# A two-byte shift in the weight conversion, and token parts of 384 and 512 in place of 448 and 448

## The chip, the cores and the metric

The kernel runs on one core of a Trainium2 chip, as one launch. The metric is the device time of that launch in microseconds (us), the median of several runs. The engines are TensorE (PE in the profile, its weight loads PEld), VectorE (DVE), ScalarE (ACT), GpSimd (POOL) and the DMA queues, most of them issued by SyncE (SP).

## The reference

Causal attention over 2 batches, 12 heads, 448 tokens and 64 columns a head is followed by two feed-forward blocks on 768 columns. Cut to what matters:

```
attn = softmax(causal(q @ k.T / 8)) @ v            # [2, 448, 768] after joining the heads
xk, xr = mixes of attn with attn of the token before (mu_k, mu_r)
k = max(xk @ w_k, 0); r = sigmoid(xr @ w_r)        # w_k [768, 1024], w_r [768, 768]
x = r * ((k * k) @ w_v)                            # w_v [1024, 768]
h = max(x @ w_in, 0)
out = (h * sigmoid(conv3(h))) @ w_out
```

The five weight matrices and `conv_w` arrive as doubles, in 64-bit words, and are narrowed to floats on the chip; all other inputs are floats.

## The kernel before

Each product of the two blocks is made of three matmuls: both operands are split into a high and a low part, and `mm3` (L64) adds high by high, high by low and low by high. The weights come slice by slice, 128 output columns wide, with all input rows (128 partitions, 768 or 1024 elements). Each slice goes through the steps of `narrow` (L132), which turn a double into a float: `a` (ACT, the high word as a float, its absolute value), `b` (a clamp, on DVE or POOL), `c` (a shift and a mask, DVE, L142), `d` (sign and top exponent bit of the high word are put in, DVE, L144) and `e` (the three top bits of the low word are put in, DVE, L146). Then `h` (ACT) and `l` (DVE or POOL) split the float. In the profile a slice's tiles are `wr1raw`, `wr1c` and `wr1hl` for slice 1 of `w_r`, and so on; there are 36 slices, and `conv_w` is narrowed in the same way as one small tile.

The token axis has 896 tokens, two batches of 448. A PSUM bank holds 512 columns. The products with `w_r` (six slices) and with the first two slices of `w_k` take the tokens by batch, `TOK` (L213): two parts of 448, each in a bank of its own. All later products of the first two matrices and those with `w_in` take them as `HALF` (L672), 512 and 384. The final product with `w_out` has 384 columns a matmul.

The order of the work on PE, ACT, DVE and POOL is written out by hand in two lists, `ORDER` (L500) and `LATE` (L712); each engine works its own entries in that order. Between the two lists (L636 to L710: the rest of `w_k`, all of `w_v`) a planner, which estimates what each instruction costs, orders the work. In `ORDER`, `j:kqT`, `j:sc`, `j:T`, `j:V` are PE's four steps of attention for head pair j (0 to 11; 0 to 5 are batch 0), and what stands between them on the other engines is copies (`kC`, `C`), scores out of PSUM (`red`), exponentials (`exp`), sums and norms (`rec`, `norm`) and the mixes (`mP`, `mD`, `mH`, `mL`, which make `xr`). `w1:d` is step `d` of weight slice 1. `pr1.0.5` is the product of `w_r` slice 1, token part 0, input chunk 5: three matmuls. It needs `xr` of that chunk, which the head pair of that number in each batch makes. `sr1.0` copies the finished bank out. `E0` to `E3` are the two first slices of `w_k` with two parts each, six chunks of three matmuls. So `w_r` has 6 x 6 x 3 = 108 matmuls in each part, and E has 36 in each.

The products of part 0 of `w_r` slices 1, 2, 0 and, in part, 3 stand between the steps of attention; the rest of `w_r` and E follow when attention is through. The last four entries of attention on PE are `10:V.b`, `10:V.a`, `11:V.b`, `11:V.a`; the last, of 20 matmuls, needs `11:C.aX`, a copy of a bank on ACT, and `11:C.aY` on DVE; `11:V.b` needs `11:C.bY`, DVE's last copy. On ACT `w5:a`, `8:mH`, `9:mP.1`, `w4:a` and `9:mP.0` stand ahead of `11:C.aX`. Step `w0:h` on ACT needs `w0:e` on DVE, and `9:kC.q` on ACT needs the transposes `9:kqT`.

Of the kernel before, what the change touches and what calls it, by code (L numbers as in the profile page):

```python
# [9 lines left out]
F32 = mybir.dt.float32  # L10
I32 = mybir.dt.int32
I64 = mybir.dt.int64
F32R = mybir.dt.float32r
AF = mybir.ActivationFunctionType
ALU = mybir.AluOpType
# [4 lines left out]
def kernel(  # L20
# [18 lines left out]
    nc = tc.nc  # L39
    B, H, S, D = q.shape  # L40
    P = 128
# [7 lines left out]
    NT = B * S  # L49
    NC = DM // P  # L50
    NF = DFF // P
    NE = DM // P
# [11 lines left out]
    def mm3(ps_out, lh, ll, rh, rl, first, last, more=False):  # L64
        for i, (x, y) in enumerate(((lh, rh), (lh, rl), (ll, rh))):
            nc.tensor.matmul(  # L66
                ps_out, x, y, start=first and i == 0, stop=last and i == 2, skip_group_check=more,
            )
# [9 lines left out]
    def copy(eng, out_, in_):  # L78
        (nc.vector.tensor_copy if eng == "v" else nc.scalar.copy)(out_, in_)  # L79

    def split_h(eng, out_, in_):
        if eng == "p":
            nc.gpsimd.tensor_scalar(out_, in_, 1.0, 1.0, ALU.mult, ALU.mult)
        elif eng == "v":
            nc.vector.tensor_copy(out_, in_)
        else:
            nc.scalar.activation(out_, in_, AF.Copy)  # L87

    def split_l(eng, out_, x, h):
        e = nc.gpsimd if eng == "p" else nc.vector  # L90
        e.tensor_tensor(out_, x, f32(h), ALU.subtract)  # L91
# [18 lines left out]

    raws = Slots(wp, "wraw", 2, [P, NF * P], I64)
    wcs = Slots(wp, "wc", 2, [P, NF * P])
    whls = Slots(wp, "whl", 4, [P, 2, NF * P], F32R)
    mslots = Slots(mixp, "m", 3, [P, 512])
# [3 lines left out]
    def in_order(ins):  # L118
        if pinned[0]:
            tc.keep_in_program_order(ins)  # L120
# [5 lines left out]
    def as_float(bits):  # L126
        return struct.unpack("<f", struct.pack("<I", bits))[0]

    def as_int(bits):
        return bits - (1 << 32) if bits >> 31 else bits  # L130

    def narrow(step, dst, raw, eng="v"):  # L132

        lo, hi = raw[:, 0::2], raw[:, 1::2]
        d = dst.bitcast(I32)
        if step == "a":
            in_order(nc.scalar.activation(dst, hi.bitcast(F32), AF.Abs))
        elif step == "b":
            e = nc.gpsimd if eng == "p" else nc.vector
            e.tensor_scalar(dst, dst, as_float(HIGH), as_float(LOW), ALU.min, ALU.max)  # L140
        elif step == "c":
            nc.vector.tensor_scalar(d, d, 3, as_int(0x3FFFFFF8), ALU.logical_shift_left, ALU.bitwise_and)  # L142
        elif step == "d":
            nc.vector.scalar_tensor_tensor(d, hi, as_int(0xC0000000), d, ALU.bitwise_and, ALU.bitwise_or)  # L144
        else:
            nc.vector.scalar_tensor_tensor(d, lo, 29, d, ALU.logical_shift_right, ALU.bitwise_or)  # L146

    def load(w, m, name, rows, raw=None):

# [53 lines left out]
    def home(tag):  # L203
        return act if tag in early else late[0]

    def big(tag, name):
        return home(tag).tile([P, 2, NT], F32R, tag=tag, name=name)

    mixed = [act.tile([P, B, S], F32, tag=f"T{c}", name=f"mixed{c}") for c in range(NC)]
    xr = [big(f"Y{c}", f"xr{c}") for c in range(NC)]  # L210
    xk = {}
    sr = {}
    TOK = [slice(b * S, (b + 1) * S) for b in range(B)]  # L213

    free = [f"b{i}" for i in range(8)]
    held = {}

    def bank(key, uses):
        tag = free.pop(0)
        t = ps.tile([P, 512], F32, tag=tag, name=key, bufs=1)  # L220
        held[key] = [tag, t, uses]
        return t

    def used(key):
        h = held[key]
        h[2] -= 1
        if not h[2]:
            free.append(h[0])
        return h[1]
# [195 lines left out]
    def mix_h(dst, m, b, eng):  # L425
        split_h("p" if eng == "p" else "s", dst[:, 0, TOK[b]], m)

    def mix_l(dst, m, b, eng):
        split_l(eng, dst[:, 1, TOK[b]], m, dst[:, 0, TOK[b]])

    def products(out_, w, x, t, n, c):
        o = slice(c * P, c * P + P)
        mm3(out_, w[0][:, 0, o], w[0][:, 1, o], x[c][:, 0, t], x[c][:, 1, t], c == 0, c == n - 1)
# [21 lines left out]
    def first_steps(s):  # L455

        if s == "L":
# [4 lines left out]
            small["r"] = cr = t[:3 * NF, 2 * P:]  # L462
            in_order(nc.gpsimd.dma_start(out=cr.bitcast(I64), in_=conv_w.rearrange("t (f p) -> (t f) p", p=P)))
            small["c"] = t[:3 * NF, P:2 * P]
# [91 lines left out]
    slices = [Slice(e) for e in range(9)]  # L556
    ones = bank("W", 1)

    def keep_warm(n):
        for _ in range(n):  # L560
            nc.tensor.matmul(ones[:, :P], ident, ident, start=True, stop=True)  # L561

    def xr_products(e, b, c):
        if c == 0:
            bank(f"pr{e}_{b}", 1)
        products(held[f"pr{e}_{b}"][1][:, :S], [slices[e].t], xr, TOK[b], NC, c)
        xr_done[e] += 1
        if xr_done[e] == B * NC:
            whls.put(e)

    def keep_sr(e, b, eng):
        if e not in sr:
            sr[e] = home(f"U{e}").tile([P, NT], F32, tag=f"U{e}", name=f"sr{e}")
        copy(eng, sr[e][:, TOK[b]], used(f"pr{e}_{b}")[:, :S])

    def xk_step(x, s, eng):
        b, c = divmod(x, NC)
        if s == "H":
            if c not in xk:
                xk[c] = big(f"X{c}", f"xk{c}")  # L580
            mix_h(xk[c], mixed[c][:, b], b, eng)
        else:
            mix_l(xk[c], mixed[c][:, b], b, eng)

    pk_banks = {}
    xr_done = [0] * NE

    def issue(token):
        what, _, eng = token.partition("/")
        if what == "W0":  # L590
            keep_warm(7)
        elif what == "Wend":
            used("W")
        elif what[:2] == "W*":
            keep_warm(int(what[2:]))
        elif what == "act2":
            actx.close()
            late.append(ctx.enter_context(tc.tile_pool(name="act2", bufs=1, reuse_waits="tile")))
        elif what[0] == "E":
            f, b = divmod(int(what[1:]), B)  # L600
            pk_banks[f, b] = bank(f"pk{f}_{b}", 1)[:, :S]
            for c in range(NC):
                products(pk_banks[f, b], [slices[NE + f].t], [xk[i] for i in range(NC)], TOK[b], NC, c)
        elif what[:2] == "pr":
            xr_products(*(int(y) for y in what[2:].split(".")))
        elif what[:2] == "sr":
            keep_sr(*(int(y) for y in what[2:].split(".")), eng)
        else:
            who, op = what.split(":")
            if who == "sm":  # L610
                first_steps(op)
            elif who[0] == "w":
                slices[int(who[1:])].step(op, eng)
            elif who[0] == "k":
                xk_step(int(who[1:]), op, eng)
            else:
                op, *a = op.split(".")
                job = jobs[int(who)]
                if op in ("Lk", "Lv"):
                    getattr(job, op)()  # L620
                else:
                    getattr(job, "T_" if op == "T" else op)(eng, *a)
# [7 lines left out]
    xk = [xk[c] for c in range(NC)]  # L630
# [11 lines left out]
    def convert_next():  # L642
# [10 lines left out]
        if i < KH:  # L653
            t = slot(F32R, f"b11_{i}")
        wo_c.append(c := convert(*x, slot(F32, f"wo{i}c").rearrange("p a b -> p (a b)")))
# [18 lines left out]
    def token_mm(name, w, x, late_):  # L674

        n = len(x)
        out_ = [next_bank(f"{name}_{b}")[:, :t.stop - t.start] for b, t in enumerate(HALF)]
        for c, b in sorted(((c, b) for b in range(B) for c in range(n)), key=lambda k: (late_ and k[0] == n - 1, k[1])):
            products(out_[b], w, x, HALF[b], n, c)
        return list(zip(HALF, out_))  # L680
# [5 lines left out]
    for f in range(NF):  # L686
        w = take()
        k2.append(big(f"Y{f}", f"k2_{f}"))
        pks = [(TOK[b], pk_banks[f, b]) for b in range(B)] if f < 2 else token_mm(f"pk{f}", w, xk, False)
        for t, pk in pks:  # L690
            a = mslots.turn(f"a{f}")[:, :t.stop - t.start]
            nc.scalar.activation(a, pk, AF.Relu)
            nc.scalar.activation(a, a, AF.Square)
            split_h("s", k2[f][:, 0, t], a)
            split_l("v", k2[f][:, 1, t], a, k2[f][:, 0, t])
        if f in (2, 5):
            convert_next()

    x2 = []
    for e in range(NE):  # L700
        x2.append(big(f"X{e}", f"x2_{e}"))
        tc.keep_in_program_order(nc.scalar.activation(sr[e], sr[e], AF.Sigmoid))
        w = take()
# [158 lines left out]
    def pair(name):  # L862
        x = pairs.pop(0)
        if isinstance(x, tuple):
            e, i = x
            if e not in st:
                st[e] = late[0].tile([P, 2, 2, WT], F32R, tag=f"X{e}", name=f"st{e}")
            x = st[e][:, i]
# [195 lines left out]
```

## Time and profile before

| | us |
|---|---|
| median of 3 runs | 354.03 |
| lowest, highest | 353.97, 354.67 |
| span of the profiled execution, first to last instruction | 351.6 |
| busy in it: PE, DVE, ACT, POOL | 345.2, 306.9, 235.1, 90.3 |

The profiled execution has no time of its own beside its span; the median of the runs lies 2.43 us above the span. Times in the profile are us from the span's start, and L144 is line 144 of the kernel. The granted TensorE clock is 1.00 (2.4 GHz) in all stretches.

The stages are: attention with the fillers named above up to 90.03; the rest of `w_r` up to 120.66; E and the rest of `w_k` up to 179.77; `w_v` up to 237.79; `w_in` with the convolution up to 297; `w_out` up to 348.3; the last copy and store.

### The profile page before, as it was taken

The numbers are of one execution on the slowest core, as the hardware profiler recorded it, in microseconds if no ns is written. First come the engines' busy times: TensorE is split into PE (matmuls) and PEld (weight loads), VectorE is DVE, ScalarE is ACT, GpSimd is POOL, SyncE is SP. The second block draws the span as 40 slices with busy tenths as digits, with TensorE's granted clock in tenths as the row PEclk, the third lists the DMA queues.
The fourth block names the chain that finished last, engine by engine and source line by source line (L and its number), as shares of the span: only waits on it lengthen the run. The fifth ranks groups of instructions, "written<-read, shape, count | busy, mean of one in ns | idle before, by whom it ended". The sixth has DMA issues, their size and how long they took to land.

```text
span 351.6 us, 7196 instructions
## 1 busy us (share of the span) xinstructions
PE 345.2 (98%) x2682; PEld 309.2 (88%) x2682; DVE 306.9 (87%) x629; ACT 235.1 (67%) x515; POOL 90.3 (26%) x149
## 2 busy tenths in 40 slices
PE   7999999999999999999999999999999999999996
PEld 7678788888999998998889999988988999999995
DVE  2999999999889878989999998997998999897741
ACT  2999999999533276767786464354756877766501
POOL 3386986667435000000000000000000000368100
PEclk9999999999999999999999999999999999999999
DMA  5686597442033155347455434543232200379623
GB/s 132 146 222 144 127 222 213 90 116 93 7 95 106 66 180 181 121 148 240 142 187 171 156 101 173 179 143 128 89 103 79 89 2 0 67 134 202 138 91 135
DMA packets 63228, 45.33 MB, mean 129 GB/s; under 512 B 34752, under 2 KB 62156, under 8 KB 63192
## 3 DMA queue, kind: packets, MB, share of 16 engines
q1 hardware_dynamic: 59352, 40.68, 38.7%
q0 software_dynamic: 2912, 3.96, 6.6%
q8 instruction: 21, 0.34, 0.4%
q10 hardware_dynamic: 928, 0.23, 0.3%
q14 instruction: 15, 0.12, 0.1%
HBM read 38.17 MB, written 2.75 MB: 116 GB/s over the span
## 4 chain that ended last, share of the span: by engine, by line
PE 95%; DVE 1%; DMA 1%; POOL 1%; SPq 1%; issue 1%; ACT 0%; POOLq 0%
PE pk L66 17%; PE pv L66 17%; PE pr L66 13%; PE A L66 7%; PE po L391 6%; PE s L321 4%; PE B L66 4%; PE c L66 2%; PE Yb L363 2%; PE D L66 2%; PE Xa L363 2%; PE W L561 1%; PE q L300 1%; PE ph5l L66 1%; PE ph6l L66 1%; PE ph4l L66 1%
## 5 line engine op out<-in xcount | busy, mean ns | idle before, releaser
L887 POOL DMA_DIRECT2D s<-g x12 | 12.7, 1177 | 194.9 <-ACT st L87 188.6
L343 ACT ACTIVATE p<-e,st 128x448 f32<-128x448 f32 (+6 forms) x84 | 42.1, 507 | 1.7 <-DVE st L334 1.5
L72 POOL TENSOR_SCALAR p<-p,st 128x64 f32<-128x64 f32 (+6 forms) x70 | 34.6, 512 | 20.7 <-DVE st L334 11.4
L334 DVE CUSTOM_DVE_ANT_0 e<-s,mask 128x192 f32<-128x192 f32 (+6 forms) x84 | 31.6, 415 | 0.4 <-ACT p L343 0.2
L391 PE MATMUL po<-pt,v 128*64 128x128 f32 (+4 forms) x384 | 24.0, 277 | 0.0
L807 DVE SCALAR_TENSOR_TENSOR cv<-hT,cw,cv 128x448 f32<-128x448 f32 x32 | 21.5, 681 | 2.7 <-ACT cv L804 2.6
L391 PEld LDWEIGHTS po<-pt,v 128*64 128x64 f32 x384 | 20.0, 137 | 3.3 <-issue 0.3
L321 PE MATMUL s<-kT,qT 64*64 64x384 f32 (+6 forms) x336 | 22.1, 386 | 0.5 <-DVE kT L79 0.2
L321 PEld LDWEIGHTS s<-kT,qT 64*64 64x64 f32 x336 | 14.9, 132 | 6.6 <-ACT qT L79 0.7
L343 ACT ACTIVATION_READ_ACCUMULATOR p<-e,st 128x1 f32 x84 | 16.3, 194 | 0.0
L91 POOL TENSOR_TENSOR xr<-m,xr 128x448 fp32r<-128x448 f32 x10 | 12.0, 1198 | 2.1 <-ACT xr L87 1.7
L87 ACT ACTIVATE x<-xv 128x512 fp32r<-128x512 f32 (+1 forms) x12 | 6.8, 573 | 8.1 <-DVE xv L706 8.0
L811 ACT ACTIVATE cv<-cv 128x448 f32<-128x448 f32 x16 | 9.1, 571 | 3.2 <-DVE cv L807 3.2
L999 ACT ACTIVATE o<-A 128x384 f32<-128x384 f32 x3 | 1.5, 491 | 14.7 <-PE A L66 14.6
L804 ACT ACTIVATE cv<-hT,cw 128x448 f32<-128x448 f32 x16 | 10.7, 668 | 0.5 <-DVE g L91 0.3
L813 DVE TENSOR_TENSOR cv<-cv,hT 128x448 f32<-128x448 f32 x16 | 9.9, 621 | 1.2 <-ACT cv L811 1.2
L91 DVE TENSOR_TENSOR k<-a,k 128x512 fp32r<-128x512 f32 (+2 forms) x16 | 9.9, 619 | 0.0
L66 PE MATMUL pv<-k,wv0hl 128*128 128x512 f32 (+1 forms) x48 | 9.9, 364 | 0.0
L66 PE MATMUL pv<-k,wv4hl 128*128 128x512 f32 (+1 forms) x48 | 9.8, 363 | 0.0
L66 PE MATMUL pv<-k,wv2hl 128*128 128x512 f32 (+1 forms) x48 | 9.8, 363 | 0.0
L66 PE MATMUL pv<-k,wv3hl 128*128 128x512 f32 (+1 forms) x48 | 9.8, 363 | 0.0
L66 PE MATMUL pv<-k,wv5hl 128*128 128x512 f32 (+1 forms) x48 | 9.8, 363 | 0.0
(516 smaller groups left out, 1105.0 us busy)
## 6 DMA issues: line engine op xcount, KB each, us to landing
rqk<-in_q_dram SPq DMA_DIRECT2D x24, 112.0 KB, 2.8
rqk<-in_k_dram SPq DMA_DIRECT2D x22, 112.0 KB, 3.0
v<-in_v_dram SPq DMA_DIRECT2D x24, 96.0 KB, 3.0
s<-g POOLq DMA_DIRECT2D x12, 192.0 KB, 3.8
wo6raw<-g POOLq DMA_DIRECT2D x8, 192.0 KB, 4.8
wv0raw<-in_moe_w_v_dram SPq DMA_DIRECT2D x1, 1024.0 KB, 4.8
wv1raw<-in_moe_w_v_dram SPq DMA_DIRECT2D x1, 1024.0 KB, 4.9
wv2raw<-in_moe_w_v_dram SPq DMA_DIRECT2D x1, 1024.0 KB, 5.0
```

The source lines that it names most:

```text
L66: nc.tensor.matmul(ps_out, x, y, start=first and i == 0, stop=last and i == 2, skip_group_check=more,)
L72: nc.gpsimd.tensor_scalar(out_, in_, s, 1.0, ALU.mult, ALU.mult)
L91: e.tensor_tensor(out_, x, f32(h), ALU.subtract)
L321: nc.tensor.matmul(held[self.name(f"s{f}")][1][h, o:z], qT[r, i * LO:(i + 1) * LO], kT[r, :(i + 1) * LO], start=True, stop=True,)
L334: nc.vector.tensor_tensor_reduce(t[:, :w], used(self.name(f"s{f}"))[:, o:z], mask[:, S - w:], -SCALE, 3e38, ALU.add, ALU.min, self.st[:, 0 ...
L343: nc.scalar.activation(p[:, :w], self.s[i][:, :w], AF.Exp, bias=self.st[:, 0, i:i + 1], scale=-1.0, accum_out=self.st[:, 1, i:i + 1],)
L363: nc.tensor.transpose(o[:, u * LO:(u + 1) * LO], self.p[i][r, k0:k0 + P], ident[r, r])
L391: nc.tensor.matmul(self.T["po"][j * D:(j + 1) * D, 1 + i * LO - z:1 + (i + n) * LO], self.v[:, kc, j], self.T["pt"][:, a - z:a + n * LO], ...
L804: nc.scalar.activation(a, x[:, 0:S], AF.Copy, scale=cw[:, f:f + 1])
L807: nc.vector.scalar_tensor_tensor(a, x[:, j:S + j], cw[:, j * NF + f:j * NF + f + 1], a, ALU.mult, ALU.add)
L813: (nc.gpsimd if eng == "p" else nc.vector).tensor_tensor(a, a, hc, ALU.mult)
L887: nc.gpsimd.dma_start(out=dst, in_=f32(x), accum_op=ALU.add)
```

## The change

In `narrow`, step `d` no longer works on the float under construction. It now takes the raw words as two-byte pieces (four to a double), shifts the upper piece of the low word right by 13, masks it to three bits and writes it over the lower piece of the high word, in place. Step `e` then takes from the high word the sign, the top exponent bit and these three bits at once. Step `d` was an instruction of two tensor sources (`scalar_tensor_tensor`) and is one of a single source (`tensor_scalar`) whose elements lie eight bytes apart; `e` remains one of two sources.

The parts of the token axis for `w_r` and for E become `PART`: 384 and 512. Entries of `ORDER` and `LATE` are the same, in the same order, and `TOK` remains where the mixes write `xr` and `xk`.

```diff
+U16 = mybir.dt.uint16
...
-        lo, hi = raw[:, 0::2], raw[:, 1::2]
+        hi = raw[:, 1::2]
...
         elif step == "d":
-            nc.vector.scalar_tensor_tensor(d, hi, as_int(0xC0000000), d, ALU.bitwise_and, ALU.bitwise_or)
-        else:
-            nc.vector.scalar_tensor_tensor(d, lo, 29, d, ALU.logical_shift_right, ALU.bitwise_or)
+            half = raw.bitcast(U16)
+            nc.vector.tensor_scalar(half[:, 2::4], half[:, 1::4], 13, 7, ALU.logical_shift_right, ALU.bitwise_and)
+        else:
+            nc.vector.scalar_tensor_tensor(d, hi, as_int(0xC0000007), d, ALU.bitwise_and, ALU.bitwise_or)
...
+    PART = [slice(0, 3 * P), slice(3 * P, NT)]
+
+    def width(t):
+        return t.stop - t.start
...
-        products(held[f"pr{e}_{b}"][1][:, :S], [slices[e].t], xr, TOK[b], NC, c)
+        t = PART[b]
+        products(held[f"pr{e}_{b}"][1][:, :width(t)], [slices[e].t], xr, t, NC, c)
...
-        copy(eng, sr[e][:, TOK[b]], used(f"pr{e}_{b}")[:, :S])
+        t = PART[b]
+        copy(eng, sr[e][:, t], used(f"pr{e}_{b}")[:, :width(t)])
...
-            pk_banks[f, b] = bank(f"pk{f}_{b}", 1)[:, :S]
+            t = PART[b]
+            pk_banks[f, b] = bank(f"pk{f}_{b}", 1)[:, :width(t)]
             for c in range(NC):
-                products(pk_banks[f, b], [slices[NE + f].t], [xk[i] for i in range(NC)], TOK[b], NC, c)
+                products(pk_banks[f, b], [slices[NE + f].t], [xk[i] for i in range(NC)], t, NC, c)
...
-        pks = [(TOK[b], pk_banks[f, b]) for b in range(B)] if f < 2 else token_mm(f"pk{f}", w, xk, False)
+        pks = [(PART[b], pk_banks[f, b]) for b in range(B)] if f < 2 else token_mm(f"pk{f}", w, xk, False)
```

## Rows read from the trace of the kernel before

**Rows 1.** The page, part 1 (busy us, share, instructions) and part 4 (chain).

```profile
PE 345.2 (98%) x2682; PEld 309.2 (88%) x2682; DVE 306.9 (87%) x629; ACT 235.1 (67%) x515; POOL 90.3 (26%) x149
PE 95%; DVE 1%; DMA 1%; POOL 1%; SPq 1%; issue 1%; ACT 0%; POOLq 0%
```

**Rows 2.** Windows: stretch, us, busy PE, PEld, DVE, ACT, POOL, clock, DMA, GB/s.

```profile
44.00:88.30 44.30, 44.30 (x668) 37.67 (x666) 43.04 (x132) 43.55 (x126) 32.74 (x50) 1.00 0.55 145
124.40:179.77 55.37, 55.37 (x274) 49.82 (x274) 48.85 (x68) 40.35 (x67) 0.00 (x0) 1.00 0.53 175
179.77:237.79 58.02, 58.02 (x289) 52.14 (x289) 54.63 (x80) 31.44 (x43) 0.00 (x0) 1.00 0.47 157
237.79:297.00 59.21, 59.21 (x295) 52.99 (x294) 54.43 (x91) 41.21 (x82) 0.00 (x0) 1.00 0.22 70
```

**Rows 3.** Chain of waits: start us, us, what, count; unbroken matmul runs.

```profile
120.66 3.72 PE pk L66 x18
237.79 4.12 PE ph0l L66 x18
242.60 3.14 PE ph0h L66 x18
179.77 58.03 PE pv L66 x288
```

**Rows 4.** Chain of waits, first and last of w_r products before 90 us.

```profile
46.34 1.41 PE pr L66 x6
79.00 3.23 PE pr L66 x15
```

**Rows 5.** Timelines of DVE and PE, 97 us.

```profile
97.00 0.61 DVE L91 TENSOR_TENSOR xr<-m,xr 128x448 fp32r<-128x448 f32 x1
97.56 1.40 PE L66 MATMUL pr<-xr,wr1hl 128*128 128x448 f32 x6
```

**Rows 6.** Timelines, 87 to 90 us: start us, us, instruction [idle before].

```profile
87.78 0.63 ACT L76 ACTIVATE mixed<-po,mu 128x448 f32<-128x448 f32 x1
88.29 0.59 ACT L79 COPY pt<-Xa 128x512 f32<-128x512 f32 x1
87.18 0.68 DVE L79 COPY pt<-Yb 128x512 f32<-128x512 f32 x1
88.84 0.56 DVE L142 TENSOR_SCALAR wr4c<-wr4c 128x768 int32<-128x768 int32 x1 [0.98 <-POOL wr4c L140]
89.04 1.06 PE L391 MATMUL po<-pt,v 128*64 128x65 f32 x20
```

**Rows 7.** Timeline of ACT: the two waits between 44 and 88 us.

```profile
48.92 0.53 ACT L79 COPY qT<-q 128x448 f32<-128x448 f32 x1 [0.32 <-PE k L300]
72.05 0.85 ACT L87 ACTIVATE wr0hl<-wr0c 128x768 fp32r<-128x768 f32 x1 [0.31 <-DVE wr0c L146]
```

**Rows 8.** Groups of ACT by form, 44 to 90 us.

```profile
L79 ACT COPY sr<-pr 128x448 f32<-128x448 f32 x2 | 1.1, 532 | 0.0
L79 ACT COPY pt<-Xa 128x512 f32<-128x512 f32 x6 | 3.5, 576 | 0.0
```

**Rows 9.** Lines 142, 144 on DVE: ns min/median/max, first, last start us.

```profile
L142 DVE TENSOR_SCALAR wr2c<-wr2c x1: 506/506/506, 54.2 to 54.2; 128x768 int32<-128x768 int32 x1
L144 DVE SCALAR_TENSOR_TENSOR wr1c<-wr1raw,wr1c x1: 951/951/951, 33.0 to 33.0; 128x768 int32<-128x768 int32 x1
L144 DVE SCALAR_TENSOR_TENSOR wr3c<-wr3raw,wr3c x1: 946/946/946, 71.9 to 71.9; 128x768 int32<-128x768 int32 x1
L144 DVE SCALAR_TENSOR_TENSOR wk0c<-wk0raw,wk0c x1: 1785/1785/1785, 107.7 to 107.7; 128x768 int32<-128x768 int32 x1
```

**Rows 10.** Groups of DVE by form: busy us, mean ns, idle before.

```profile
L91 DVE TENSOR_TENSOR wi0hl<-wi0c,wi0hl 128x768 fp32r<-128x768 f32 x1 | 1.0, 951 | 0.0
```

**Rows 11.** Timeline of POOL beside the slow DVE instruction at 107.7 us.

```profile
107.27 3.27 POOL L91 TENSOR_TENSOR xk<-mixed,xk 128x448 fp32r<-128x448 f32 x2
```

**Rows 12.** Line 144 on DVE, 179.77 to 237.79 us: the waits ahead.

```profile
L144 DVEq EVENT_SEMAPHORE  x11: 21/21/21, 181.0 to 235.4; - x11
```

## The prediction

> **What bounds the kernel now.** I read the page first. PE is busy for 345.2 of 351.6 us and makes 95% of the chain that ended last [rows 1], so a matmul that gets shorter should shorten the kernel. A busy PE is only an average, though, so next come the windows. In the stages behind attention PE has no idle time, while DVE has 6.52, 3.39 and 4.78 us of it (stretch less busy time) and ACT more [rows 2]: there PE alone is the bound. In 44.00 to 88.30, the part of attention that contains the first `w_r` products, all three are full: PE 44.30, DVE 43.04, ACT 43.55 of 44.30 us [rows 2]. The reader is to see that the idle time of ACT there is 0.75 us. PE waits for nothing in that stretch, yet it has little room: whatever shortens PE's work there is worth only what ACT and DVE can follow.
>
> **The token parts: matmuls.** Prices come from unbroken runs. 448 columns: 18 in 3.72 us, 206.7 ns each. 512: 18 in 4.12 us, 228.9 ns. 384: 18 in 3.14 us, 174.4 ns [rows 3]. So a matmul of part 0 loses 32.3 ns and one of part 1 gains 22.2 ns. There are 108 of `w_r` and 36 of E in each part: 144 x (32.3 - 22.2) = 1.45 us less PE work in all. The mixed stage agrees: 58.03 us for 288 matmuls is 403 ns for a pair [rows 3], against 413.4 for two of 448.
>
> The places count. Before 90.03 only part 0 of `w_r` is worked: six runs, from 46.34 to 82.23 us, of 6 to 15 matmuls, 66 in all [rows 4]. They lose 66 x 32.3 ns = 2.13 us. Behind 90.03 come the other 42 of part 0 (-1.36), 108 of part 1 (+2.40) and E (36 x -32.3 and 36 x 22.2 ns: -0.36). That sum is +0.68 us. PE's stream from 90.03 on becomes 0.68 us longer, and PE is the bound from there to the end, so the kernel changes by 0.68 us less S, where S is how much earlier PE gets through with attention.
>
> Could PE wait in its new stream behind 90.03? The tightest entry that I find is `pr1.1.5`, which starts at 98.18 (half of the six from 97.56), while DVE's `11:mL` ends at 97.61 [rows 5]: 0.57 us of room. The 13 entries ahead of it are 12 of part 1 and one of part 0, so it starts 12 x 0.067 - 0.097 = 0.70 us later by width and S earlier. No wait while S is below 1.27.
>
> **What ACT allows.** ACT's last copy for attention, `11:C.aX`, runs from 88.29 to 88.88 with the work before it right ahead; PE's `11:V.a`, which needs it, starts at 89.04 [rows 6]. The room is 0.16 us, of which I take 0.10. DVE's last copy ends at 87.86, and DVE then idles 0.98 us [rows 6], so ACT sets the end. S is then 0.10 plus what ACT comes earlier, and ACT comes earlier only where it idled or where its own work shrinks:
>
> - `9:kC.q` waited 0.32 us for PE's transposes [rows 7]. Six matmuls lie before it: 6 x 32.3 ns = 0.19.
> - `w0:h` waited 0.31 for DVE's `w0:e` [rows 7]. It goes if DVE comes 0.5 us earlier there (next part): 0.31.
> - The other 0.12 of the idle time: I take 0.08.
> - Two copies `sr` of 448 columns take 532 ns each, one of 512 takes 576 [rows 8]: 64 columns fewer are 44 ns, twice 0.09.
>
> Together S = 0.77. From both sides: all of ACT's idle time, its copies and all of the room are 0.75 + 0.09 + 0.16 = 1.00; the first wait kept and half of the room gives about 0.45. Filling PE's remaining lead is what was cost at nothing: of the 2.13 us, some 1.4 us turn into waits of PE for ACT and DVE.
>
> **The conversion.** Step `e` keeps its form. Step `d` at 768 elements takes 951 ns [rows 9], and a dense instruction of two sources takes the same 951 ns [rows 10], so every-second-word reading costs nothing visible. The new `d` has the engine, operation and width of `c`, which takes 506 ns [rows 9], but steps of eight bytes and pieces of two bytes, which no row of before writes. Bounds: 506 ns below, 951 ns if it runs at one element at a time, and above that the slowest row of `d`, 1785 ns [rows 9], which ran beside POOL's subtractions [rows 11]. I take 0.51, the row of its own operation. The Trainium skill ("VectorE: DVE Perf Modes", section "What auto-detection actually checks") gives a one-source operation within SBUF two elements at a time and names no step for that mode; by it the price is that of `c`, and no row here shows it for stepped pieces.
>
> So each `d` saves 0.44 us. Four of them lie before 88 us, from 33.0 to 71.9 [rows 9], three of these ahead of `w0:e`: 1.3 us, enough for the 0.5 that ACT asks for even where DVE in turn waits. Behind attention the saving lies beside PE's full rows and is worth nothing. The new `d` writes the raw tile that ACT's `a` reads, but in the lists it stands behind `b` and `c`, which wait for `a` anyway, so no wait is added; `e` stays the last reader, and the load that follows isn't held longer. In the stretch between the lists the planner may put `d` ahead of `b`; with 6.52 and 3.39 us of idle DVE [rows 2] that is cost at nothing.
>
> **The sum.** Span: +0.68 - 0.77 = -0.09 us, 351.5. The runs lie 2.43 above the span; nothing at either end changes. 354.03 - 0.09 = 353.9 us. With S between 0.45 and 1.00 the forecast's own range is 353.7 to 354.3.
>
> **Rivals.**
>
> A. PE alone binds, and ACT and DVE follow it: all of 1.45 us is won, 352.6. For it: no wait of PE from 44 to 90 and a chain of PE throughout [rows 1]. Against: 0.75 us of idle ACT [rows 2], and 0.16 us of room at the end [rows 6].
>
> B. Slower: the stepped two-byte write costs more than the old `d`. Half way between 951 and 1785 ns it is 1.37 us, +0.42 each. In attention four of them are 1.68 us on DVE, whose idle time up to 87.86 is 0.82 (43.04 busy, 0.44 of the 1.26 lies behind) [rows 2, 6]: PE ends attention 0.86 later, and S is -0.86. In the `w_v` stage 11 conversions [rows 12] add 4.6 us to a DVE with 3.39 idle, 1.2 more. 354.03 + 0.68 + 0.86 + 1.2 = 356.8. It decides from about 1.16 us a piece in attention (0.82 / 4 above the old) and 1.26 in the `w_v` stage. For it: no row shows such a write. Against: stepped reads are free. The Trainium skill ("Vector Engine (DVE) Microarchitecture Reference", section "Measured stream behaviour on trn2") speaks for it: a port runs at full rate only over pairs of adjacent four-byte words, and a destination that hops at each element takes 1.71 ns a column, by which 768 columns would be an estimated 1.3 us. The stepped reads of the old `d` don't agree with that rule (951 ns, as dense); its stepped writes are open.
>
> C. The new `d` is no faster than the old. Then `w0:h` still waits for DVE, what ACT gained before 72 us is lost there, and S is 0.10 + 0.04 (one `sr` copy behind it) + 0.05 = 0.2: 354.03 + 0.68 - 0.2 = 354.5. This is also how the conversion's edit would fail to do what it is for.
>
> **Chances.** Forecast 0.45, A 0.15, B 0.17, C 0.17, and 0.06 for what I don't see, a worse order by the planner first of all. A measurement of this kernel can tell 0.2%, 0.71 us, from no change. Faster by more: A and a little of the forecast, 0.17. Slower by more: B, the upper part of C (0.04) and most of the rest, 0.25. Between: 0.58. The range that leaves out 2 in 10 reaches over A and C, and leaves most of B and A's lower half: 352.5 to 355.3.
>
> **What would show it.** In the profile after: matmuls of `pr` at 174 and 229 ns in runs; PE idle in 46 to 90 us, about 1.4 us in all, ended by ACT or DVE; `11:V.a` through at 89.2 to 89.4 in place of 90.10; E's first matmul at about 121.0 (120.66, with 39 of part 0 and 108 of part 1 ahead of it +1.14, less 0.77); `d` at about 0.51 us; the wait of `w0:h` gone; PE full in all later windows. The prediction is wrong if PE still doesn't wait before 90 us and attention ends 2 us earlier (A), if `d` takes over 1.16 us (B) or about 0.95 (C), or if PE idles behind 125 us.

## The result and the profile after

The changed kernel takes 357.36 us (median of 4 runs, 357.00 to 357.71) against 354.15 for the kernel before: ratio 1.009, interval 1.0075 to 1.0104. It is slower by 3.2 us, where 353.9 and a range up to 355.3 were predicted. Ratios here are worked from the undisturbed runs and need not be the quotient of the medians, which are over all runs.

The page of the changed kernel, parts 1 and 4, answers to [rows 1]:

```profile
PE 347.4 (98%) x2682; PEld 308.7 (87%) x2682; DVE 305.6 (86%) x629; ACT 234.8 (66%) x515; POOL 90.5 (25%) x149
...
PE 39%; DVE 20%; DMA 9%; ACT 5%; issue 2%; SPq 0%; ACTq 0%
```

PE was 95% of the chain and is 39% now: DVE, loads and ACT, which were 2% together, stand on it for 34%, so something in the weights' path sets the pace. Where, the windows by stage tell (columns as in [rows 2]; first a part of attention, then E with the rest of `w_k`, then `w_v`, then `w_in`):

```profile
44.90:89.20 44.30, 43.59 (x671) 37.53 (x672) 43.15 (x132) 43.46 (x125) 32.87 (x50) 1.00 0.54 146
...
122.67:181.42 58.75, 58.75 (x293) 52.85 (x293) 52.81 (x75) 41.61 (x67) 0.00 (x0) 1.00 0.53 171
181.42:240.92 59.50, 58.53 (x290) 52.07 (x289) 49.87 (x74) 30.48 (x42) 0.00 (x0) 1.00 0.45 149
240.92:300.85 59.93, 59.50 (x293) 52.65 (x292) 57.00 (x96) 41.40 (x83) 0.00 (x0) 1.00 0.21 67
```

Length by length, against the same stages of before:

| stage on PE | before | after | |
|---|---|---|---|
| attention, first to last `po` | 69.31 | 69.24 | -0.07 |
| rest of `w_r`, E, `w_k` (to 179.77; to 181.42) | 89.67 | 90.36 | +0.69 |
| `w_v` (to 237.79; to 240.92) | 58.02 | 59.50 | +1.48 |
| `w_in` (to 296.76; to 300.85) | 58.97 | 59.93 | +0.96 |
| to the end of the span | 54.83 | 54.87 | +0.04 |

These are 3.10 us. (`po` is PE's product of probabilities and values; first to last `po` is attention.) The first `po` also lies 1.03 us later in this span than in that of before. Where it lies differs from run to run (0.41 to 1.18 us later than before in the runs below), so I count stages and medians, not it. The time of a run lies 1.7 to 1.9 us above its own span wherever both are known; the 2.43 for the kernel before compares a median with the span of another execution.

Of `w_v`'s 1.48 us, 0.97 are waits of PE (59.50 less 58.53), and of `w_in`'s 0.96, 0.43. The other 0.5 in each is PE busy for longer at a clock of 1.00. There are two waits in each stage, and the first matmul behind a wait runs alone: 0.44 us for 384 columns and 0.49 for 512 (rows below) against 174 and 229 ns each in a run. By these rows a wait costs an estimated 0.27 us beside its length.

The first `w_v` products end in a wait of PE for ACT's last split of `k2_7`, the last eighth of what `w_v` is multiplied with. Timeline of PE, then of ACT, in the changed kernel (start, us, instruction, idle before it and what ended that):

```profile
187.82 2.77 PE L67 MATMUL pv<-k,wv0hl 128*128 128x384 f32 x14
191.40 0.44 PE L67 MATMUL pv<-k,wv0hl 128*128 128x384 f32 x1 [0.81 <-ACT k L88]
```

```profile
183.47 0.92 ACT L138 ACTIVATE wo2c<-wo2raw 128x768 f32<-128x768 f32 x1 [1.74 <-DMA wo2raw<-in_moe_w_out_dram]
...
187.43 0.51 ACT L702 ACTIVATE a<-a 128x384 f32<-128x384 f32 x1
188.15 0.53 ACT L88 ACTIVATE b<-wo2c 128x384 fp32r<-128x384 f32 x1 [0.21 <-DVE wo2c L148]
188.69 1.28 ACT L711 ACT_TABLE_LOAD   x1
189.99 0.95 ACT L711 ACTIVATE sr<-sr 128x896 f32<-128x896 f32 x1
190.84 0.51 ACT L88 ACTIVATE k<-a 128x384 fp32r<-128x384 f32 x1
```

The reader is to see a queue: the last row is what PE waits for. Its data were there at 187.94, but ahead of it stand a split of `wo2c` that waits for DVE's `e`, a table load and the sigmoid of slice 2; further ahead, ACT has sat 1.74 us for the load of `wo2`. In the kernel before, the split of `k2_7` stood ahead of all four and ended at 183.43:

```profile
182.91 0.53 ACT L87 ACTIVATE k<-a 128x384 fp32r<-128x384 f32 x1
183.45 1.28 ACT L702 ACT_TABLE_LOAD   x1
```

Neither list of the kernel says so: it is the planner's stretch, and the planner gave the changed kernel another order. Of the 150 instructions of DVE that it places, 120 stand in other places, of ACT's 114, 87, and of SP's 11, 2; those of PE and POOL don't.

The second place is the start of `w_in`, which needs `xv5`, the product of the last `w_v` slice with its sigmoid. DVE, then PE, and DVE in the kernel before:

```profile
240.76 0.56 DVE L141 TENSOR_SCALAR wi4c<-wi4c 128x768 f32<-128x768 f32 x1 [0.88 <-ACT wi4c L138]
...
242.30 1.03 DVE L146 TENSOR_SCALAR wi4raw<-wi4raw 128x768 uint16<-128x768 uint16 x1
243.12 0.72 DVE L715 TENSOR_TENSOR xv<-pv,sr 128x512 f32<-128x512 f32 x1
```

```profile
244.56 0.49 PE L67 MATMUL ph0l<-x,wi0hl 128*128 128x512 f32 x1 [0.19 <-ACT x L88]
245.28 0.73 PE L67 MATMUL ph0l<-x,wi0hl 128*128 128x512 f32 x2 [0.23 <-DVE x L92]
```

```profile
235.26 0.68 DVE L706 TENSOR_TENSOR xv<-pv,sr 128x512 f32<-128x512 f32 x1
```

The first half of `xv5` starts 2.2 us after PE's last `w_v` product (before: 2.5 us ahead of it), because `b`, `c` and `d` of `wi4` and a subtraction stand in front, and `b` itself waits 0.88 us for ACT's `a`. Here DVE isn't full: part of that time it stands idle, with `xv5` behind the instruction that waits.

The new `d` itself, line 146 on DVE (ns min/median/max, first and last start), against [rows 9]:

```profile
L146 DVE TENSOR_SCALAR wr1raw<-wr1raw x1: 1035/1035/1035, 34.0 to 34.0; 128x768 uint16<-128x768 uint16 x1
L146 DVE TENSOR_SCALAR wk0raw<-wk0raw x1: 2004/2004/2004, 109.3 to 109.3; 128x768 uint16<-128x768 uint16 x1
...
L146 DVE TENSOR_SCALAR wv0raw<-wv0raw x1: 1345/1345/1345, 163.7 to 163.7; 128x1024 uint16<-128x1024 uint16 x1
```

It takes 1.04 us, 0.09 more than the old one, not 0.44 less. The idle DVE time with which I covered the planner's order is gone ahead of the first place:

```profile
163.10:188.10 25.00, 25.00 (x126) 22.55 (x125) 25.00 (x33) 19.21 (x30) 0.00 (x0) 1.00 0.55 185
```

From `wv0`'s `b` to the `e` that ACT waits for, DVE (its busy time is the 25.00 with 33 instructions) has no idle time at all. Before, across the same border, it had some:

```profile
161.50:184.50 23.00, 23.00 (x115) 20.57 (x114) 21.73 (x28) 18.03 (x27) 0.00 (x0) 1.00 0.53 174
```

### The profile page after: what moved, and what is told of

Same layout as the page of the kernel before. It is cut to its first block, busy times and chain, and to the rows that moved or that the text cites. A ratio compares the mean times of both kernels' runs of the same rounds, so it can differ in the third digit from the quotient of the medians.

```text
span 355.7 us, 7160 instructions
## 1 busy us (share of the span) xinstructions
PE 347.4 (98%) x2682; PEld 308.7 (87%) x2682; DVE 305.6 (86%) x629; ACT 234.8 (66%) x515; POOL 90.5 (25%) x149
## 4 chain that ended last, share of the span: by engine, by line
PE 39%; DVE 20%; DMA 9%; ACT 5%; issue 2%; SPq 0%; ACTq 0%
PE pr L67 8%; PE A L67 7%; PE B L67 4%; PE c L67 2%; PE D L67 2%; DMA wv0raw<-in_moe_w_v_dram 1%; DMA wk7raw<-in_moe_w_k_dram 1%; DMA wk3raw<-in_moe_w_k_dram 1%; DMA wi1raw<-in_moe_w_in_dram 1%; DMA wi0raw<-in_moe_w_in_dram 1%; DMA wo0raw<-in_moe_w_out_dram 1%; DMA wi2raw<-in_moe_w_in_dram 1%; DVE k L92 1%; PE ph5l L67 1%; PE ph6l L67 1%
## 5 line engine op out<-in xcount | busy, mean ns | idle before, releaser
L67 PEld LDWEIGHTS pv<-k,wv0hl 128*128 128x128 f32 x48 | 8.6, 188 | 2.6 <-ACT k L88 1.3
L92 DVE TENSOR_TENSOR k<-a,k 128x384 fp32r<-128x384 f32 (+1 forms) x16 | 9.8, 617 | 1.1 <-ACT k L88 1.1
L701 ACT ACTIVATE a<-pk 128x384 f32<-128x384 f32 (+1 forms) x16 | 8.5, 531 | 3.2 <-PE pk L67 3.2
```

The costliest lines, as they stand in the source:

```text
L67: nc.tensor.matmul(ps_out, x, y, start=first and i == 0, stop=last and i == 2, skip_group_check=more,)
```

## The experiments

Two theories came first. O: the planner's new order costs some 2.4 us. D: the dearer `d` does, in any order. The edits of the first four:

```diff
@@ e1, step d (e likewise as before) @@
-            nc.vector.tensor_scalar(half[:, 2::4], half[:, 1::4], 13, 7, ALU.logical_shift_right, ALU.bitwise_and)
+            nc.vector.scalar_tensor_tensor(d, hi, as_int(0xC0000000), d, ALU.bitwise_and, ALU.bitwise_or)
@@ e2 @@
-    PART = [slice(0, 3 * P), slice(3 * P, NT)]
+    PART = TOK
@@ e3, sigmoids of w_v in the order of the slices @@
+        with tc.issue_after(sig.ins) if e else ExitStack():
+            sig = nc.scalar.activation(sr[e], sr[e], AF.Sigmoid)
@@ e4, step d, between the lists; x is the new d, traced behind c @@
+                tc.keep_in_program_order(x)
```

**e1, the parts alone.** 

> The two token parts alone; the conversion is that of before. Theory O (order): the loss of 3.2 us is 0.7 us of longer PE work behind attention, and some 2.4 us of waits of PE where w_v and w_in begin, made by the planner's new order of DVE and ACT around the new step d. Then the parts alone cost what the old conversion lets them cost: 354.15 + 0.68 less about 0.2 in attention = 354.6 us, and PE doesn't wait at the start of w_v. Theory D (duration): the new d takes 1.04 us in place of 0.95, some 38 times, and DVE is too full for it in any order; then the parts alone give 354.6 too. Theory P (parts): the 384 and 512 columns of the first two tiles of w_k by themselves change the planner's order, and PE waits: 355.5 or more.

354.78 against 354.55, ratio 1.0008 (0.9996 to 1.002); PE waits at neither place. The planner's order had changed here too (83 instructions of DVE and 43 of ACT in other places) and did no harm: P falls, and an order isn't dear only for being another one. Attention takes 69.16 us, 0.15 less than before.

**e2, the shift alone.** 

> The new conversion alone; the tokens stay 448 and 448. Theory O: the planner's order on ACT at the start of w_v is nearly that of the changed kernel (a sigmoid of slice 2 and its table load ahead of the last split of k2_7), so PE waits there: 357.36 less 0.5 to 0.7 = 356.7 us. Theory D: 356.7 as well, with the loss spread over all stages. Theory P: 354.2 to 355.

358.85, ratio 1.0112 (1.0084 to 1.0139): the loss is in the conversion. PE waits 2.19 and 0.80 us for `k2_7` at the start of `w_v`; attention takes 69.41. More than either theory gave; not spread over the stages, as D had it. Of the 4.97 us that `w_v` takes longer than before, 2.99 are these waits; behind them the granted clock was 0.50 (1.2 GHz) from 194 to 196 us, where it is 1.00 in the changed kernel.

**e3, the sigmoids held.** 

> The changed kernel with each sigmoid of w_v queued on ACT behind the one of the slice before it, so that the table load and the sigmoid of slice 2 can't stand ahead of the last split of k2_7. Nothing else is held. Theory O: PE's wait of 0.96 us in the first w_v products goes or shrinks, 1.0 to 1.4 us less: 356.0 to 356.4 us. Theory D: the last split comes late because DVE is late, so nearly nothing changes: 357.2 to 357.4.

360.28, ratio 1.0161 (1.0132 to 1.0189): a miss, dearer than the changed kernel. The wait at `w_v` did go (that stage is 58.1 us again), but at `w_in` PE now waits longer:

```profile
245.89 0.49 PE L67 MATMUL ph0l<-x,wi0hl 128*128 128x512 f32 x1 [2.92 <-ACT x L88]
```

One instruction put right moves the loss to the next handover, the next place where PE needs another engine's last piece. Four of the six executions have a mean clock of 0.990 to 0.995, the other two, at 1.00, took 358.74 and 358.86: still dearer. **e4, `d` behind `c`.** 

> The changed kernel with the new step d queued behind step c of the same slice, as the old d was by its operands. Theory O: the planner's order comes nearer to that of before (last split of k2_7 ahead of the table load), PE's wait at the start of w_v shrinks by about 1 us, the one at the start of w_in stays, since the same DVE order stands there: 356.2 to 356.6 us. Theory D: d takes as long as before in its new place: 357.2 to 357.5.

362.04, ratio 1.0207 (1.0183 to 1.023): a miss as well. PE waits 0.25 us at `w_v` and 3.47 at `w_in`, and after that wait the clock was half:

```profile
246.73:250.00 3.27, 3.27 (x7) 2.35 (x8) 3.27 (x6) 2.49 (x6) 0.00 (x0) 0.50 0.00 0
```

It was 1.00 again from 253 on. That stage takes 6.71 us longer than before, of which the clock is an estimated 3 (half of the 6.1 us at 0.50). With `d` behind `c` as before, the planner's order still differs from that of before, so the place of `d` alone doesn't explain the planner's change of order.

So the whole order had to be set. Each instruction between the lists gets the one that stood ahead of it on its engine, in another kernel, as its predecessor (issue order only, no wait):

```diff
+    ISSUE = {ET.DVE: "...", ET.Activation: "...", ET.SP: "..."}   # names, in the other kernel's order (e6, e7, e9, e13: PE's too)
...
+        for x, y in zip(names, names[1:]):
+            tc.add_manual_dep(traced[y], x, NoSync, reason="issue order")
```

**e5, the change in the order of before.** 

> The changed kernel, both parts of the change in it, with every engine's instructions issued in the order of the kernel before (the new d in the place of the old d). Theory O (order): what the planner's new order costs is gone; left are the parts (354.55 + 0.2, as they measured alone) and d's extra 0.09 us a piece, most of it beside idle DVE time: 354.5 to 355.4 us, with PE waiting less than 0.3 us where w_v and w_in begin. Theory D (duration): the dearer d is what delays DVE, so the waits come back in any order: 357 us or more.

354.67 against 354.15, ratio 1.0012 (1.0002 to 1.0023): 2.7 of the 3.2 us are gone with both parts of the change still in. O holds, and D in its strict form (in any order) falls. The three stages behind E's start, PE full in each (first two numbers):

```profile
122.06:180.81 58.75, 58.75 (x293) 52.84 (x293) 52.09 (x73) 41.15 (x67) 0.00 (x0) 1.00 0.50 166
180.81:238.84 58.03, 58.03 (x289) 52.15 (x289) 53.34 (x78) 31.46 (x43) 0.00 (x0) 1.00 0.46 148
238.84:297.81 58.97, 58.97 (x292) 52.75 (x292) 55.46 (x93) 41.05 (x83) 0.00 (x0) 1.00 0.24 78
```

**e6, the old kernel in the order of after.** 

> The kernel before, old conversion and 448 and 448 tokens, with every engine's instructions issued in the order of the changed kernel; only c and d of a slice trade places on DVE, since the old d needs c's result. Theory O: the order alone makes PE wait where w_v or w_in begins: 356 us or more, most likely about 357. Theory D: the old d keeps DVE early enough: 354.3 to 355.0.

360.10, ratio 1.0172 (1.0143 to 1.0201). The kernel before, nothing changed but the order (`c` and `d` trade places in it), waits at the same place for the same queue (ACT, then PE):

```profile
188.81 0.53 ACT L87 ACTIVATE b<-wo2c 128x384 fp32r<-128x384 f32 x1 [0.28 <-DVE wo2c L146]
189.35 1.28 ACT L702 ACT_TABLE_LOAD   x1
190.65 0.95 ACT L702 ACTIVATE sr<-sr 128x896 f32<-128x896 f32 x1
191.50 0.51 ACT L87 ACTIVATE k<-a 128x384 fp32r<-128x384 f32 x1
```

```profile
192.06 0.44 PE L66 MATMUL pv<-k,wv0hl 128*128 128x384 f32 x1 [2.72 <-ACT k L87]
```

Of the 4.95 us that `w_v` takes longer, the clock is an estimated 1.5: it was 0.50 from 193 to 196 us, half of which is lost.

**e7, the parts where PE alone binds.** In `xr_products` and `keep_sr` the parts hold from slice 4 on, and for E; the conversion is the old one, the order that of before.

```diff
+    def part(e, b):
+        return (PART if e > 3 else TOK)[b]
```

> The kernel before in its own order and with its own conversion, with the parts of 384 and 512 only where PE alone is the bound: the slices 4 and 5 of w_r and the two tiles of w_k, all worked behind attention. 72 pairs of matmuls, 10.1 ns each: 0.72 us less PE work behind attention, none of it paid back. Theory O: 354.55 - 0.7 = 353.8 us. Rival H (handover): at the start of w_v or w_in PE waits for the last split anyway, and comes 0.7 us earlier to a wait: 354.4 to 354.6.

353.75 against 354.15, ratio 0.9983 (0.9973 to 0.9994): 0.6 us faster by the ratio, 0.4 by the medians; H falls. **e12, the same with the planner left free.** 

> The kernel of e7 (parts of 384 and 512 for slices 4 and 5 and the two tiles of w_k only, old conversion) with the planner left free. With the parts alone and the planner free (e1) PE didn't wait anywhere. Theory O: so here, and the gain of 0.6 to 0.7 us stays: 353.4 to 353.9 us. Rival: the new widths move the planner to an order that costs some of it: 354.1 or more.

353.34 against 354.31, ratio 0.9977 (0.9964 to 0.9989): the rival falls, and like e7 this version beats both kernels. From the end of attention to the end of `w_k` it takes 88.92 us (30.17 and 58.75), 0.75 less than before's 89.67 and 1.44 less than the changed kernel, with PE full:

```profile
90.50:120.67 30.17, 30.17 (x147) 27.20 (x148) 27.68 (x39) 12.58 (x21) 11.31 (x11) 1.00 0.25 79
120.67:179.42 58.75, 58.75 (x293) 52.84 (x293) 50.45 (x71) 40.70 (x67) 0.00 (x0) 1.00 0.50 163
```

**e8, the price of `d` by itself.** All eight forms are one shift and mask of 768 elements, appended to the kernel before:

```diff
+        sh = lambda o, i: nc.vector.tensor_scalar(o, i, 3, 7, ALU.logical_shift_right, ALU.bitwise_and)
+        sh(hx[:, 2:4 * W:4], hx[:, 1:4 * W:4])     # two bytes: stepped, stepped
+        sh(hx[:, :W], hx[:, :W])                   # dense, dense
+        sh(hy[:, :W], hx[:, 1:4 * W:4])            # stepped read, dense write
+        sh(hx[:, 2:4 * W:4], hy[:, :W])            # dense read, stepped write
...
```

> The kernel before with eight one-source shift-and-mask instructions of 768 elements at its very end, three times over: two-byte stepped by eight bytes on both sides (the new d), two-byte dense on both sides, stepped read with dense write, dense read with stepped write, and the same four for four-byte words with a step of eight bytes (the last one dense, as step c). Theory W: the stepped write alone takes d from 0.5 to 1.04 us; then dense and stepped-read forms take about 0.5. Theory R: a step on either side does; then only the dense forms take 0.5. Theory U: the two-byte type itself does; then the dense two-byte form takes 1.0 as well. The total time says nothing: some 15 to 25 us longer.

Timeline of DVE, in that order; the last four are the same with four-byte words:

```profile
348.89 1.02 DVE L1038 TENSOR_SCALAR wo7raw<-wo7raw 128x768 uint16<-128x768 uint16 x1 [2.08 <-DMA out_dram<-wo7raw]
349.95 0.36 DVE L1038 TENSOR_SCALAR wo7raw<-wo7raw 128x768 uint16<-128x768 uint16 x1
350.34 0.56 DVE L1038 TENSOR_SCALAR wo6raw<-wo7raw 128x768 uint16<-128x768 uint16 x1
350.94 1.02 DVE L1038 TENSOR_SCALAR wo7raw<-wo6raw 128x768 uint16<-128x768 uint16 x1
351.99 0.56 DVE L1038 TENSOR_SCALAR wo7raw<-wo7raw 128x768 int32<-128x768 int32 x1
352.47 0.55 DVE L1038 TENSOR_SCALAR wo6raw<-wo7raw 128x768 int32<-128x768 int32 x1
353.06 0.56 DVE L1038 TENSOR_SCALAR wo7raw<-wo6raw 128x768 int32<-128x768 int32 x1
353.65 0.56 DVE L1038 TENSOR_SCALAR wo6raw<-wo6raw 128x768 int32<-128x768 int32 x1
```

One execution, the eight forms three times over with the same prices. W holds: only the stepped write of two-byte pieces takes 1.02. A stepped read, and a stepped write of four-byte words, cost nothing beside the dense form.

**e9, a cheap `d` in the order of before.**

```diff
-            nc.vector.tensor_scalar(half[:, 2::4], half[:, 1::4], 13, 7, ALU.logical_shift_right, ALU.bitwise_and)
+            nc.vector.tensor_scalar(lo, lo, 29, 7, ALU.logical_shift_right, ALU.bitwise_and)     # lo = raw[:, 0::2]
```

> The kernel of e5 (both parts of the change, issue order of before) with a cheaper d: the low word of each pair is shifted in place by a four-byte instruction of the same place and width, which took 0.56 us when measured by itself, in place of 1.04. What it leaves out: the three bits no longer reach the result. This is the price that the prediction took for d (0.51). Theory F (the forecast's own chain): then ACT stops waiting for w0:e, attention ends on PE 0.5 to 0.8 us earlier than in e5, counted from PE's first product of probabilities and values to its last (69.2 us there), and the time is 353.9 to 354.2. Theory A (ACT full): attention's other bounds keep it, that stretch of PE gets 0 to 0.2 us shorter, and the time is 354.5 to 354.7.

354.81 against 354.31, ratio 1.0006 (0.9994 to 1.0018). ACT's wait for `w0:e` is gone, as the forecast's chain had it, but attention is only 0.23 us shorter than in e5 (68.98; F had 0.5 to 0.8, A 0 to 0.2), and PE has a wait of 0.61 us at a place where it waits 0.07 at most in the kernels with a dear `d`. POOL, DVE and PE there, and last DVE in e5:

```profile
39.62 1.14 POOL L92 TENSOR_TENSOR xr<-m,xr 128x448 fp32r<-128x448 f32 x1
```

```profile
39.74 1.04 DVE L356 TENSOR_SCALAR st<-st 128x7 f32<-128x7 f32 x1
```

```profile
44.87 0.24 PE L369 MATMUL Xa<-ident,p 64*128 64x64 f32 x1 [0.61 <-DVE st L340]
```

```profile
39.33 0.16 DVE L356 TENSOR_SCALAR st<-st 128x7 f32<-128x7 f32 x1
```

A DVE instruction of 7 elements (0.16 us in e5, where it starts 0.05 us ahead of POOL's) ends with POOL's subtraction. Whether attention would have given the predicted 0.77 us without that collision isn't shown. On time the run is closer to A, but its interval reaches into both theories.

**e10 and e11, the order of before on one engine alone.** ISSUE holds only ACT's names, or only DVE's. 

> The changed kernel with the issue order of before on ACT alone; DVE keeps 111 of 553 instructions in other places than before. Theory: the order on DVE starts it. ACT in its old order then waits for DVE where DVE does other things first, the wait at the start of w_v or of w_in stays, and the time is 356.5 to 360 us. Rival: ACT's order (table load and sigmoid ahead of the last split) is what costs: 354.5 to 355.4.

> The changed kernel with the issue order of before on DVE alone; 21 of 439 instructions of ACT stand elsewhere than before. Theory: with DVE in order ACT's last split of k2_7 comes in time, and nothing waits: 354.5 to 355.2 us, as in e5. Rival: the order of ACT is what costs: 356 or more.

e10: 354.94, ratio 1.0016 (1.0003 to 1.0028), no wait of PE behind attention, though 111 instructions of DVE stand in the new places. My theory falls there, its rival holds: with ACT in its old order the new one on DVE does no harm. e11: 355.23, ratio 1.003 (1.0017 to 1.0042), just above what my theory gave; ACT's order at the start of `w_v` comes back with DVE's, and 0.29 us of PE's wait is left there. In its profile attention takes 69.99 us, 0.75 more than in the changed kernel, with a wait of PE of 0.61 at 54.76 that the other runs don't have. In both runs, then, ACT works its old order but for 21 instructions in e11; a run with ACT alone in the new one wasn't made.

**e13, a cheap `d` in the order of after.** The `d` of e9 (0.56 us), the changed kernel's order. 

> The kernel of e9 (four-byte shift of 0.56 us in place of the new d's 1.04, both parts; the three bits don't reach the result) issued in the order of the changed kernel instead of that of before. Theory N (the order is bad in itself): PE waits at the start of w_v or w_in as in the changed kernel: 356.5 us or more. Theory Q (the order is good for a cheap d and falls apart only because the real d is dear): with d at about the price that I predicted nothing waits: 354.3 to 355.2 us.

354.77 against 354.17, ratio 1.002 (1.001 to 1.003). The same queue stands on ACT, with the last split of `k2_7` behind the sigmoid, but it starts 8.31 us after PE's end of `w_k` in place of 9.42, and PE waits 0.11 us for it in place of 0.81. Q holds, N falls. DVE, and ACT's row:

```profile
160.00:186.70 26.70, 26.70 (x133) 23.75 (x132) 22.60 (x34) 19.94 (x31) 0.00 (x0) 1.00 0.52 168
```

```profile
189.41 0.51 ACT L88 ACTIVATE k<-a 128x384 fp32r<-128x384 f32 x1
```

DVE (22.60 busy of 26.70) has 4.10 us to spare where it had none. The planner's order fits a cheap `d` and falls behind with the real one.

## Why the prediction was wrong

**Where it failed: the price of `d`, "I take 0.51".** It is 1.04, inside the bounds that the prediction named (0.506 to 1.785), and nearer to the row of the old `d` than to that of `c`, which was chosen. With `d` at 0.56 in the changed kernel's own order the time is 354.77 (e13), with 1.04 it is 357.36. Of its signs of being wrong, PE idle behind 125 us is the one that came.

**What made 0.5 us a piece so dear: "that is cost at nothing", of the planner's order.** The idle DVE time behind it (6.52 and 3.39 us, [rows 2]) was a sum over stages of 55 and 58 us; in the 23 us across their border DVE had 1.27 us (21.73 busy of 23.00, 161.50 to 184.50 before), and now, in 25 us there, none. And the order puts ACT's last split behind work that hangs on DVE. What was cost at nothing measured 1.48 us in `w_v` and 0.96 in `w_in`. Price and order make it only together: the dear `d` in the order of before costs 0.1% (e5), the cheap `d` in the new order 0.2% (e13), both 0.9%. Rival B reckoned this stage with the sum of DVE's idle time alone and put its turning point at 1.26 us a piece; it lies below 1.04 in this order, in which the old `d`, at 0.95, loses too (e6). That its 356.8 comes near the 357.36 is luck: it has `d` at 1.37 and 0.86 of the loss in attention, where nothing was lost. Why the planner chose the order isn't measured; that it fits a `d` of half the time is shown, that it reckoned with one is only argued.

**Right: the matmuls.** From the end of attention to the end of `w_k` PE takes 0.69 us longer; 0.68 was predicted, and E's two runs of 18 show the widths (the next matmul starts 3.12 and 4.13 us after the first: 173 and 229 ns each):

```profile
122.67 3.28 PE L67 MATMUL pk<-xk,wk0hl 128*128 128x384 f32 x18
...
126.31 4.28 PE L67 MATMUL pk<-xk,wk0hl 128*128 128x512 f32 x18
```

**Wrong in size: S.** Attention takes 0.07 us less, not 0.77. ACT sets the end, as argued: PE waits 0.08 us for its last copy. But PE's other waits there, 0.45 and 0.26 us (the 0.71 of 44.90 to 89.20), end with DVE, and the wait of `w0:h` for DVE (0.31 of S) could not go with `d` at 1.04 and is longer now:

```profile
73.19 0.85 ACT L88 ACTIVATE wr0hl<-wr0c 128x768 fp32r<-128x768 f32 x1 [0.38 <-DVE wr0c L148]
```

With the cheap `d` that wait is gone, and still S is 0.33 in e9 and 0.27 in e13, both with the collision described there. Rival C, a `d` no faster than the old, gave S = 0.2 and 354.5: that is e5 (0.10 in its trace, 354.67). Had the order been kept, C would have been the answer. Rival A falls: of its 1.45 us the parts alone win nothing (e1). The chance of 0.06 for "a worse order by the planner" was the one that came, far too small for an edit that gives a planner's instruction other operands.

The page that I cited for the other side, the Trainium skill's "Vector Engine (DVE) Microarchitecture Reference" (section "Measured stream behaviour on trn2"), gave an estimated 1.3 us for 768 stepped writes, from its figure for hops of 4 KiB; the 1.02 of e8 is nearer to it than my 0.51, but four-byte stepped writes take 0.56 in e8, so its rule as I used it doesn't agree with these rows.

## What to carry to other kernels

Where a planner orders the work, an edit can change the order of much else, and the edited instruction's price is only the start: compare the queues of both programs, and look for a split or a copy that PE needs behind something that waits for another engine. Idle time summed over a stage is no cover; ask for it in the stretch ahead of each handover. Count a wait of PE for more than its length, since the clock can fall with it (e2, e4, e6). And put a shorter matmul where PE is the bound: the same parts, used only behind attention, gain 0.2%, used everywhere 0.

## What the runs showed of the hardware

- On DVE a one-source instruction of 768 elements takes 0.36 us for dense two-byte elements, 0.56 for four-byte words, stepped or dense, 0.56 when it reads two-byte elements eight bytes apart and writes them densely, and 1.02 when it writes them eight bytes apart (e8).
- A DVE instruction of 7 elements took 1.04 us in place of 0.16 when it started 0.12 us behind a POOL subtraction of 1.14 us, and ended with it (e9; again 1.05 in e13). The Trainium skill ("SBUF — State Buffer", section "Who interferes with whom") says that a DVE instruction in a two-port mode and a GpSimd instruction exclude each other, and the one that comes second waits for the whole of the first; the rows agree in that, and no row shows the mode.
- The granted clock fell from 1.00 to 0.50 (2.4 to 1.2 GHz) during or just behind PE's waits of 2.19 and 0.80 us in e2, 2.72 in e6 and 3.47 in e4, for some 3 us in the first two and 6 in e4; e3's profile has a wait of 2.92 with no such fall. In the changed kernel, with no wait above 0.81 behind attention, it is 1.00 throughout.
